# Mirrored spectral weights by a gather from GpSimd in place of a mirrored copy in DRAM, in a two-layer spectral and FFN kernel

## The chip, the cores and the metric

The kernel runs on one core of one Trainium2 chip. The metric is device time in microseconds, the median of several runs. A profiled execution is one further run; its span is the time between the first and the last recorded event on the core.

## The reference

The input x has 2048 rows (positions) of 448 features in bf16. Two kinds of layer alternate, A, B, A, B, each with a residual:

```
x = x + A(layernorm(x));  x = x + B(layernorm(x))      # twice, same weights
A(x):  X = rfft2(x);  X = X * (w_r + 1j*w_i);  return irfft2(X)      # w: [2048, 225]
B(x):  h = relu(x @ w1 + b1)**2;  return h @ w2 + b2                 # 448 -> 1792 -> 448
```

The rfft runs over the features (225 frequencies, number 0 is not needed here because the layernorm takes out the mean), the full FFT over the 2048 positions. The weights of A are indexed by position frequency k (2048 rows) and feature frequency l.

## The kernel before, in words

**Stages of A.** The 2048-point transform is split as 32 x 64. Stage A (`first_A`, `second_A`) multiplies 16 tiles of 128 positions by a small matrix `FA` that also carries the layernorm's 1/std, and gives the components of 32 residues in `XA`. Because the input is real, residue k1 and residue 32-k1 are conjugates, so that the stages after it work on 16 pairs p: residues p and 32-p, and for p=0 the residues 0 and 16. The groups of pairs (`GROUPS`, one or two pairs each) go through four steps:

- `stage_TD`: the transform over the features, by `TD_sb` in the first layer and, on half the length, by `TQ_sb` in the second; every product needs all 16 tiles in `XA`. The result is copied from PSUM into `U`.
- `stage_B`: the 64-point transform with twiddle factors, by the table `G_sb`; copied into `EF`, as residue p and residue 32-p side by side.
- `stage_W`: the complex multiplication by the weights, on VectorE: two products (`tmp` <- `EF` times `Wa`, and times `Wb`), then a sum and a difference into `Z`.
- `stage_Bi`: the inverse 64-point transform by the table `H_sb`, copied into `VT`.

`stage_TI` and `stage_AI` go back over the features and the residues and add the residual, `ln_B` computes the second layernorm, a DMA transpose gives `yT`, and `h_rows` and `o_tile` are the FFN. Then the second layer follows.

**The weights.** `Wa` holds real over imaginary parts on the two halves of the partitions, `Wb` the other way round. Partition q holds rows 32q+k of w. For the residue 32-p, row 32-p is needed and q runs backwards. So the kernel before first writes a mirrored copy of half the weights to DRAM, `Wrev` (16 x 64 rows of 224), with two DMAs on SP, and `load_W` then reads rows p from w and rows 32-p from `Wrev`, in rows of 224 bf16, 448 bytes. It does that in three `RANGES` of p, with G and H cut in the same way, all from SP's queue. The weights lie in buffers that are otherwise `x_sb` and `xin` (`Wa` of first and second layer) and `yT` (`Wb`), so that they are loaded anew for the second layer, in between the transposes of the FFN.

**The order of the work.** The author's `_Sched` records every operation with its reads and writes, gives each engine a list order from assumed costs, priorities (`PR`) and choices of engine (`EN`: a letter per step, `a` ScalarE, `d` VectorE, `p` GpSimd, other letters a choice), and puts in semaphore waits. The engines then follow their lists strictly. DMAs on SP made before `sch.chain = None` keep the order in which they are written. `warm_fn` puts products of ones where PE would stand.

**Lines of the profile.** L577 is every matrix product, L617, L618 are copies on ScalarE and on VectorE or GpSimd, L635 is every VectorE operation on two tensors (the weights' products among them), L572 every plain DMA, L567 the transposes, L1104 the products of ones. `DIRECT` names pairs that skip the sum and difference in `stage_W` and use twice as many products in `stage_Bi` in their place: 14 and 15 in the second layer. In the profile `xr` appears as `VT`, `U`, `EF`, `Z` and the FFN's hidden rows as `arena`, `Wb` as `yT`, the first `Wa` as `x_sb`, the second as `xin`.

Of the kernel before, what the change touches and what calls it, by code (L numbers as in the profile page):

```python
# [10 lines left out]
P = 128  # L11
S = 2048
D = 448
# [10 lines left out]
DIRECT = ((), (14, 15))  # L24
GROUPS = ((1,), (0,), (2, 3), (4, 5), (6, 7), (8, 9), (10, 11), (12, 13), (14, 15))
RANGES = ((0, 4), (4, 10), (10, 16))
# [10 lines left out]
def make_constants():  # L37

    comp = np.zeros((32, 32))
    hi = np.arange(32)
    comp[0] = 1.0
    comp[1] = np.cos(np.pi * hi)
    for p in range(1, 16):
        comp[2 * p] = np.cos(2 * np.pi * p * hi / 32)
        comp[2 * p + 1] = -np.sin(2 * np.pi * p * hi / 32)
    FA = np.zeros((32, 4, 32, 4))
    for j in range(4):
        FA[:, j, :, j] = comp.T  # L50
    FA = FA.reshape(P, P)
    FI = FA.T.copy()

    dd = np.arange(HD)[:, None]
    l = np.arange(1, 225)[None, :]
    th = 2 * np.pi * l * (dd - 223.5) / D  # L60
    TD = np.zeros((2, 2, P, LW))
    for g, M in enumerate((np.cos(th), -np.sin(th))):
        TD[g, 0] = M[:P]
        TD[g, 1, 32:] = M[P:]
    TD = TD.transpose(2, 0, 1, 3)


    th = 2 * np.pi * np.arange(1, 225)[None, :] * (np.arange(QD)[:, None] - 223.5) / D
    TQ = np.zeros((QD, 2, 2, QD))
    for g, M in enumerate((np.cos(th), -np.sin(th))):  # L70
        TQ[:, g, 0] = M[:, 1 - g::2]
        TQ[:, g, 1] = M[:, g::2]


    m = np.arange(64)
    lo = (m % 4) * 16 + m // 4
    k2 = np.arange(64)
    G = np.zeros((P, NP, 2, 192))
    H = np.zeros((P, NP, 2, 256))
    for p in range(NP):  # L80
        for q in range(2):
            k = (p if p or not q else 16) + 32 * k2
            th = 2 * np.pi * lo[:, None] * k[None, :] / float(S)
            c, n = np.cos(th), np.sin(th)
            if p:
                C, Dm = np.concatenate([c, n]), np.concatenate([-n, c])
            else:
                z = np.zeros_like(c)
                C, Dm = (np.concatenate([a, z] if q == 0 else [z, a]) for a in (c, -n))
            G[:, p, q] = np.concatenate([-Dm, C, Dm] if p == 0 or q == 0 else [Dm, C, -Dm], 1)  # L90
            K, N = c.T, n.T
            if p:
                b = np.concatenate([-N, K, N, -K], 1)
                H[:, p, q] = np.concatenate([b, -b if q == 0 else b])
            else:
                for g, b in enumerate((np.concatenate([K, N], 1), np.concatenate([-N, K], 1))):
                    H[:, p, g, q * P:(q + 1) * P] = np.concatenate([b, -b if g == 0 else b])


    l0 = np.arange(1, 225)[:, None]  # L100
    cl = np.where(l0 == 224, 1.0, 2.0) / (S * D)
    th = 2 * np.pi * l0 * (np.arange(HD)[None, :] - 223.5) / D
    TI = np.zeros((QD, 2, 2, HD))
    for g, M in enumerate((cl * np.cos(th), cl * np.sin(th))):
        for r in range(2):
            TI[:, r, g] = M[r::2]

    return dict(FA=np.concatenate([FA, -FA], 1), FI=np.concatenate([FI, -FI], 1), TD=TD, G=G, H=H, TI=TI, TQ=TQ,
                J=np.eye(P)[::-1])
# [82 lines left out]
def _pages(ap):  # L192
# [12 lines left out]
    p0 = ap.offset // row if row else 0  # L205
    halves = range(p0 // 64, (p0 + pat[0][1] - 1) // 64 + 1)
    return [(name, int(i), h) for i in pg for h in halves]


class _Sched:  # L210

    ENGINES = ("pe", "act", "dve", "pool", "sp")
    NDSEM = {"sp": 20, "pool": 16, "act": 8, "pe": 0, "dve": 0}
    DMA_RATE = 400.0
    SWITCH = 95.0
    STICK = 3000.0

    def __init__(self):
        self.ops = {e: [] for e in self.ENGINES}
        self.units = []
        self.last_write = {}
        self.reads_since = {}
        self.bias = 0.0
        self.look = dict.fromkeys(self.ENGINES, 0.0)
        self.chain = None
        self.warm_fn = None
# [5 lines left out]
    def add(self, eng, fn, reads=(), writes=(), is_dma=False, cost=100.0, lat=130.0, unit=None):  # L235
# [22 lines left out]
        if unit is not None:  # L258
            u = unit
        elif tile is not None and tile.unit is not None:  # L260
            u = tile.unit
        else:
            u = _Unit(eng, tile)
            u.bias = self.bias
            u.seq = len(self.units)
            if is_dma and eng == "sp" and self.chain is not None:
                u.after, self.chain = self.chain or None, u
            self.units.append(u)
            if tile is not None:
                tile.unit = u  # L270
# [30 lines left out]
    def schedule(self):  # L301
# [32 lines left out]
        cand = {e: [] for e in self.ENGINES}  # L334
        bank_free = [0.0] * NB
        bank_user = [None] * NB
        dma_free = 2300.0

        ready = {}
        best = {}  # L340
# [154 lines left out]
def bass_interleave_layers__spectral_gfnet__dense_activation_squared_relu__prompt_kernel(nc, A_x, A_w_r, A_w_i, B_x, B_w1, B_b1, B_w2, B_b2, out):  # L495
# [6 lines left out]
    with ExitStack() as es:  # L502
# [179 lines left out]
        def load_W(W, f, p0, p1):  # L682

            for i in range(2):
                rows, w = slice(64 * (i ^ f), 64 * (i ^ f) + 64), w_dram[i]
                dma("sp", W[rows, p0:p1, 0, :], w[:, p0:p1, 1:225])
                if p0 == 0:
                    dma("sp", W[rows, 0:1, 1, :], w[:, 16:17, 1:225])
# [494 lines left out]
```

## Time and profile before

| | us |
|---|---|
| median of 9 runs | 278.81 |
| lowest and highest | 277.25, 280.34 |
| profiled execution | 278.24 |
| span of its profile | 276.4 |
| busy PE | 259.1 (94%) |
| busy PE, loading weights | 168.7 (61%) |
| busy DVE (VectorE) | 206.8 (75%) |
| busy ACT (ScalarE) | 176.9 (64%) |
| busy POOL (GpSimd) | 9.6 (3%) |

PE is TensorE. Matmuls overlap, so a busy PE isn't PE at its best rate. HBM was read for 18.02 MB and written for 2.75 MB. In the profile `[5.03 <-DMA X]` after an instruction is the time for which its engine stood idle before it and what ended that time; a line of waits gives who waited, for whom, the sum, the number of times and the longest. A chain of waits follows the work that ended last back to what released it.

### The profile page before, as it was taken

The numbers are of one execution on the slowest core, as the hardware profiler recorded it, in microseconds if no ns is written. First come the engines' busy times: TensorE is split into PE (matmuls) and PEld (weight loads), VectorE is DVE, ScalarE is ACT, GpSimd is POOL, SyncE is SP. The second block draws the span as 40 slices with busy tenths as digits, with TensorE's granted clock in tenths as the row PEclk, the third lists the DMA queues.
The fourth block names the chain that finished last, engine by engine and source line by source line (L and its number), as shares of the span: only waits on it lengthen the run. The fifth ranks groups of instructions, "written<-read, shape, count | busy, mean of one in ns | idle before, by whom it ended". The sixth has DMA issues, their size and how long they took to land.

```text
span 276.4 us, 6385 instructions
## 1 busy us (share of the span) xinstructions
PE 259.1 (94%) x2385; PEld 168.7 (61%) x2385; DVE 206.8 (75%) x686; ACT 176.9 (64%) x366; POOL 9.6 (3%) x23
## 2 busy tenths in 40 slices
PE   7699669999998999999999999899999999999995
PEld 2479647879654444554458799769754554554454
DVE  3876467599999999898689698599999865212542
ACT  5797826899747976324815789899856795001820
POOL 2740000000000000000000000000000000000000
PEclk9799968999999999999999999999999999999999
DMA  7969999902233424202230400002332600111001
GB/s 236 311 143 264 279 219 314 318 4 47 62 54 69 82 38 105 55 0 63 52 88 6 96 2 4 0 4 40 21 75 62 142 2 8 42 50 36 0 23 46
DMA packets 42969, 23.92 MB, mean 87 GB/s; under 512 B 35164, under 2 KB 41660, under 8 KB 42940
## 3 DMA queue, kind: packets, MB, share of 16 engines
q1 hardware_dynamic: 41996, 22.77, 34.1%
q10 hardware_dynamic: 944, 0.75, 0.8%
q8 instruction: 19, 0.31, 0.5%
q14 instruction: 10, 0.08, 0.1%
HBM read 18.02 MB, written 2.75 MB: 75 GB/s over the span
## 4 chain that ended last, share of the span: by engine, by line
PE 66%; SPq 13%; DVE 7%; ACT 7%; DMA 3%; issue 2%; DVEq 0%; ACTq 0%
PE ps L577 66%; SPq L572 13%; ACT VT L617 3%; DMA yT<-Wrev 2%; ACT tmp L617 2%; ACT arena L617 2%; DVE tmp L635 1%; DMA yT<-xin 1%; DVE x_sb L912 1%; DVE x_sb L910 1%; ACT yT L617 1%; DVE arena L635 1%; DVE xin L644 1%; DVE XA L618 0%; DVE st L928 0%
## 5 line engine op out<-in xcount | busy, mean ns | idle before, releaser
L600 ACT ACTIVATE arena<-ps,b1T 128x512 bf16<-128x512 f32 (+1 forms) x140 | 73.7, 615 | 30.8 <-PE ps L577 30.6
L577 PE MATMUL ps<-yT,W_sb 64*128 64x512 bf16 (+1 forms) x980 | 86.1, 333 | 1.2 <-DMA yT<-xin 0.9
L577 PE MATMUL ps<-W_sb,arena 128*128 128x448 bf16 (+1 forms) x476 | 87.1, 341 | 0.0
L577 PEld LDWEIGHTS ps<-yT,W_sb 64*128 64x128 bf16 x980 | 49.8, 94 | 37.2 <-issue 1.8
L577 PEld LDWEIGHTS ps<-W_sb,arena 128*128 128x128 bf16 x476 | 46.0, 98 | 37.2 <-DVE arena L635 0.8
L635 DVE TENSOR_TENSOR arena<-arena 128x512 bf16<-128x512 bf16 (+1 forms) x140 | 47.9, 367 | 15.4 <-ACT arena L600 15.1
L1009 DVE TENSOR_TENSOR x_sb<-ps,arena 128x448 bf16<-128x448 f32 (+1 forms) x34 | 20.2, 595 | 23.7 <-PE ps L577 23.4
L617 ACT ACTIVATE arena<-ps 128x896 bf16<-128x896 f32 (+1 forms) x32 | 25.9, 865 | 11.2 <-PE ps L577 11.2
L600 ACT ACTIVATE mv<-mv,epst 128x2 f32<-128x2 f32 (+1 forms) x42 | 12.1, 298 | 21.0 <-DVE mv L737 19.3
L577 PE MATMUL ps<-arena,G_sb 128*128 128x224 bf16 x128 | 16.7, 285 | 5.0 <-DMA G_sb<-c_G 5.0
L716 ACT ACTIVATE VT<-x_sb 128x448 bf16<-128x448 bf16 x24 | 13.7, 570 | 11.1 <-DVE x_sb L912 11.1
L577 PE MATMUL ps<-H_sb,arena 128*128 128x128 bf16 x272 | 17.9, 224 | 0.7 <-DVE arena L635 0.6
L577 PEld LDWEIGHTS ps<-H_sb,arena 128*128 128x128 bf16 x272 | 16.7, 101 | 1.6 <-DVE arena L635 1.5
L577 PEld LDWEIGHTS ps<-arena,G_sb 128*128 128x128 bf16 x128 | 13.2, 108 | 6.3 <-DMA G_sb<-c_G 5.3
L617 ACT ACTIVATE VT<-ps 128x512 bf16<-128x512 f32 x29 | 15.4, 644 | 1.9 <-PE ps L577 1.8
L635 DVE TENSOR_TENSOR arena<-tmp 128x896 bf16<-128x896 bf16 (+1 forms) x30 | 16.2, 587 | 0.1
L617 ACT ACTIVATE XA<-ps 128x512 bf16<-128x512 f32 x25 | 13.9, 598 | 3.5 <-PE ps L577 3.5
L617 ACT ACTIVATE tmp<-ps 128x896 bf16<-128x896 f32 (+1 forms) x18 | 14.3, 850 | 2.2 <-PE ps L577 2.2
L1104 PE MATMUL ps<-ones 128*128 128x512 bf16 x40 | 12.3, 436 | 2.0 <-POOL ones L648 1.9
L635 DVE TENSOR_TENSOR tmp<-arena,yT 128x896 bf16<-128x896 bf16 (+1 forms) x15 | 8.7, 588 | 6.2 <-DMA yT<-Wrev 6.2
L644 DVE TENSOR_SCALAR xin<-x_sb,mv,rstd 128x512 bf16<-128x512 bf16 x32 | 11.6, 405 | 0.0
L577 PE MATMUL ps<-Fs,xin 128*128 128x256 bf16 x32 | 9.0, 303 | 2.5 <-POOL Fs L629 2.2
(74 smaller groups left out, 262.9 us busy)
## 6 DMA issues: line engine op xcount, KB each, us to landing
W_sb<-in_B_w_dram SPq DMA_DIRECT2D x2, 896.0 KB, 10.1
out_dram<-x_sb SPq DMA_DIRECT2D x15, 112.0 KB, 1.7
W_sb<-in_B_w_dram SPq DMA_DIRECT2D x1, 1568.0 KB, 14.2
H_sb<-c_H SPq DMA_DIRECT2D x2, 768.0 KB, 7.7
yT<-Wrev SPq DMA_DIRECT2D x8, 168.0 KB, 5.2
G_sb<-c_G SPq DMA_DIRECT2D x2, 576.0 KB, 8.3
xin<-in_A_x_dram SPq DMA_DIRECT2D x2, 448.0 KB, 5.7
x_sb<-Wrev SPq DMA_DIRECT2D x4, 168.0 KB, 8.9
```

Of the source, the lines that this page charges most:

```text
L572: return e.dma_start(o, i)
L577: op = sch.add("pe", lambda e: e.matmul(_res(o), lhsT, rhs, start=start, stop=stop, skip_group_check=skip), [lhsT, rhs], [o], cost=max(_fr ...
L600: sch.add("act", lambda e: e.activation(o, _res(i), func, **kw), rd, [o], cost=c)
L617: op = sch.add("act", lambda e: e.activation(o, _res(i), ACT.Copy) if h[0].eng == "act" else e.tensor_copy(o, _res(i)), [i], [o], cost=c[" ...
L635: sch.add(eng, lambda e: e.tensor_tensor(o, _res(a), b, op), [a, b], [o], cost=_free(o) / rate + 69.0)
L644: sch.add(eng, lambda e: e.tensor_scalar(o, i, s1, s2, op0=op0, **kw), rd, [o], cost=_free(o) / 3.84 + 50.0 + (10.0, 80.0, 140.0)[len(rd) ...
L716: sch.add("act", lambda e: e.activation(o, x, ACT.Square, accum_out=sd[:, t, 1:2]), [x], [o, sd[:, t, 1:2]], cost=560.0)
L910: sch.add("dve", lambda e, xx=xx, xi=xi, r=r: e.tensor_tensor(xx, _res(r), xi, ALU.add), [r, xi], [xx], cost=536.0)
L912: small(lambda e, xx=xx, xi=xi, r=r, i=i: e.scalar_tensor_tensor(out=xx, in0=_res(r), scalar=1.0, in1=xi, op0=ALU.mult, op1=ALU.add, accum ...
L1009: sch.add("dve", lambda e: e.tensor_tensor(o, _res(i), xb[:, t, d0:d1], ALU.add), [i, xb[:, t, d0:d1]], [o], cost=(d1 - d0) / 0.96 + 69.0)
L1104: return lambda e: e.matmul(ps[:, b, :], ones[:], ones[:, None, :].to_broadcast([P, 4, P]), start=True, stop=True)
```

## The change

- `Wrev` and its two DMAs go. `load_W` now copies whole runs of consecutive rows, `WC` = 225 elements each, into one row of 33 slots per partition, and gets the mirrored rows by `gather`: an indirect DMA from GpSimd, each of 64 partitions by 8 rows of w (1800 elements), whose row numbers come from the constant list `back` (63 down to 0, times 4, plus 3 or 2). Eight gathers load the first layer's weights, eight the second's.
- Since runs of w aren't turned about in p, the mirrored residues of a group stand in reverse: `stage_B` writes them so, `stage_W` reads the weights with a hand-built access pattern and turns them back in the sum and difference. Rows start at p x 225 + 1, so every other one starts at an odd element.
- G has one table per p, shared by both residues (192 columns, not 2 x 192), H 384 columns (not 512). `DIRECT` is gone. p=0 goes last, there are two `RANGES`.
- In the second layer `stage_TD` writes adjacent PSUM columns, and the copy to `U` interleaves them (before: a step of 2 in PSUM).
- FA comes first on ACT's DMA queue, J and b1 come after the first range. `A2`'s scratch moves from `xin` to `VT`. All of `PR` and `EN` and some assumed costs are new, so that each engine's order is new too. On GpSimd the first eight gathers now stand between the reversed copies of tiles 10 and 11 and of tiles 6 and 7.

```diff
-DIRECT = ((), (14, 15))
-GROUPS = ((1,), (0,), (2, 3), (4, 5), (6, 7), (8, 9), (10, 11), (12, 13), (14, 15))
-RANGES = ((0, 4), (4, 10), (10, 16))
+GROUPS = ((1,), (2, 3), (4, 5), (6, 7), (8, 9), (10, 11), (12, 13), (14, 15), (0,))
+RANGES = ((1, 6), (6, 16))
+WC = 225
+HQ = 384
...
+    dc["back"] = nc.inline_tensor((4 * (63 - m) + np.array([[3, 2]])).astype(np.uint32), name="c_back").ap()
...
-        G_sb = sb("G_sb", [P, NP, 2, 192])
-        H_sb = sb("H_sb", [P, NP, 2, 256])
+        G_sb = sb("G_sb", [P, NP + 1, 192])
+        H_sb = sb("H_sb", [P, 15 * HQ + 4 * P])
...
+        def gather(o, i, h):
+            idx = bass.IndirectOffsetOnAxis(back[:, h:h + 1], 0)
+            sch.add("pool", lambda e: e.indirect_dma_start(o, None, i, idx), [back[:, h:h + 1]], [o], is_dma=True, cost=1000.0,
+                    lat=2.0 * 64 * 8 * WC / sch.DMA_RATE)
...
-        Wrev = [nc.dram_tensor(f"Wrev{i}", (16, 64, LW), BF16, kind="Internal").ap() for i in range(2)]
-        for i in range(2):
-            dma("sp", Wrev[i], (A_w_r, A_w_i)[i].rearrange("(q k) l -> k q l", k=32)[16:32, ::-1, 1:225], writes=[f"Wrev{i}"])
...
+            a, b = (0, p1) if p0 == 1 else (p0, 17)
             for i in range(2):
-                rows, w = slice(64 * (i ^ f), 64 * (i ^ f) + 64), w_dram[i]
-                dma("sp", W[rows, p0:p1, 0, :], w[:, p0:p1, 1:225])
-                if p0 == 0:
-                    dma("sp", W[rows, 0:1, 1, :], w[:, 16:17, 1:225])
+                dma("sp", W[64 * (i ^ f):64 * (i ^ f) + 64, a * WC:b * WC], w_dram[i][:, a * WC:b * WC])
+            h = 0 if p0 == 1 else 1
             for i in range(2):
-                rows = slice(64 * (i ^ f), 64 * (i ^ f) + 64)
-                r, p = Wrev[i].rearrange("k r l -> r k l"), max(p0, 1)
-                dma("sp", W[rows, p:p1, 1, :], r[:, 16 - p:16 - p1:-1, :], reads=[f"Wrev{i}"])
+                j = 64 * (1 - (i ^ f))
+                gather(W[j:j + 64, WC * (25 - 8 * h) + 1:WC * (33 - 8 * h) + 1], w_rows[i], h)
...
-                            l0 = g * LW + ((1 - g) if k == 0 else g)
-                            o, x, w = slice(l0, l0 + LW - 1, 2), x[0:QD], TQ_sb[:, g, k, :]
+                            l0 = 256 * g + QD * ((1 - g) if k == 0 else g)
+                            o, x, w = slice(l0, l0 + QD), x[0:QD], TQ_sb[:, g, k, :]
...
-                tt(T[:, f], X, W[:, p:p + n], ALU.mult)
+                a = W[:, p * WC + 1:p * WC + 1 + LW]
+                a = bass.AP(tensor=a.tensor, offset=a.offset, ap=[list(a.ap)[0], [WC, n], [WC * (34 - 2 * p - n) + 1 if p else WC * 16, 2],
+                                                                  [1, LW]])
+                tt(z.rearrange("p q (f s) l -> p f q s l", f=2)[:, f] if p == 0 else T[:, f], X, a, ALU.mult)
...
-            tt(z[:, 0:2], T[:, :, :, 0], T[:, :, :, 1], ALU.add)
-            tt(z[:, 2:4], T[:, :, :, 0], T[:, :, :, 1], ALU.subtract)
+            for i, op in enumerate((ALU.add, ALU.subtract)):
+                tt(z[:, 2 * i:2 * i + 2], T[:, :, :, 0], T[:, :, ::-1, 1], op)
...
-                        w = xin[:, t, 0:D].rearrange("p (g d) -> p g d", g=2)
+                        w = VT[:].rearrange("p a b t c j -> p (a b t c j)")[:, 512 * t:512 * t + D].rearrange("p (g d) -> p g d", g=2)
```

## The prediction, made before the changed kernel ran

> **What bounds the kernel now.** I read the 40 slices first, for a resource that is full while PE is not:
>
> ```profile
> PE   7699669999998999999999999899999999999995
> ...
> DMA  7969999902233424202230400002332600111001
> GB/s 236 311 143 264 279 219 314 318 4 47 62 54 69 82 38 105 55 0 63 52 88 6 96 2 4 0 4 40 21 75 62 142 2 8 42 50 36 0 23 46
> DMA packets 42969, 23.92 MB, mean 87 GB/s; under 512 B 35164, under 2 KB 41660, under 8 KB 42940
> ```
>
> A slice is 6.9 us. For the first eight, up to 55 us, the transfers are full and PE has its only deep hole (a 6); after that PE is at 9 and DMA idles. 35164 of 42969 packets are under 512 bytes: the rows of weights are 448. Next the waits from 20 to 60 us, for who stands in the hole:
>
> ```profile
> DVE tmp L635 <- DMA yT<-Wrev: 6.2, 2, 3.5
> PEld ps L577 <- DMA G_sb<-c_G: 5.3, 1, 5.3
> PE ps L577 <- DMA G_sb<-c_G: 5.0, 1, 5.0
> ```
>
> Then PE's timeline, first stage and (from 154.19) second stage, for what the hole costs:
>
> ```profile
> 29.77 2.46 PE L577 MATMUL ps<-TD_sb,XA 128*128 128x224 bf16 x24
> 37.27 4.66 PE L577 MATMUL ps<-arena,G_sb 128*128 128x224 bf16 x24 [5.03 <-DMA G_sb<-c_G]
> 41.72 3.59 PE L577 MATMUL ps<-H_sb,arena 128*128 128x128 bf16 x48
> ...
> 51.75 1.69 PE L577 MATMUL ps<-TI_sb,VT 112*128 112x224 bf16 x16 [0.46 <-ACT VT L617]
> ...
> 154.19 2.46 PE L577 MATMUL ps<-TQ_sb,XA 112*128 112x112 bf16 x24 [0.33 <-DVE XA L618]
> ...
> 176.84 1.32 PE L577 MATMUL ps<-TI_sb,VT 112*128 112x224 bf16 x16 [0.45 <-ACT VT L617]
> ...
> 180.00 0.95 PE L577 MATMUL ps<-TI_sb,VT 112*128 112x112 bf16 x16
> 180.89 0.93 PE L577 MATMUL ps<-tmp,FI_sb 128*128 128x448 bf16 x4
> ```
>
> After the 5.03 us wait the 24 G products start 190 ns apart; undisturbed ones start 97 ns apart. The windows say why: the granted clock is 0.58 and 0.50 of full in 36 to 42 us. So a starved PE pays twice. The first spectral stage, from its first TD product (21.21 us) to the first TI (51.75), takes 30.5 us; the second, whose weights are already on the chip, 154.19 to 176.84, **22.65 us**. The difference, 7.9 us, is the transfers' price.
>
> What bounds the second stage? Its two windows, with busy us of PE, PEld, DVE, ACT, POOL, then clock, DMA share and GB/s:
>
> ```profile
> 154.20:165.00 10.80, 10.80 (x125) 10.80 (x126) 8.87 (x18) 8.53 (x12) 0.00 (x0) 1.00 0.07 16
> 165.00:176.80 11.80, 10.76 (x153) 9.54 (x150) 9.43 (x17) 11.47 (x20) 0.00 (x0) 1.00 0.01 2
> ```
>
> PE first, then ACT (11.47 of 11.80): near balance, so one engine relieved gains little, and in stage one ACT is what is late next once the transfers are gone.
>
> **What the Trainium skill says.** "DMA: Bandwidth & Descriptors", Specifications: line rate needs transfers of at least 512 B. The trace agrees: 193 to 272 GB/s at a DMA share of 1.0 in 33 to 42 us, where 448-byte rows move, against 386, 380 and 341 in 45 to 54 us with long rows. The same page, same table: a DMA from GpSimd has its first byte after about 1 us, one from SP about 0.6; and, Anatomy of one DMA, about 2.0 us fixed for the whole transfer. No run here has a DMA from GpSimd. "GPSIMD Engine Reference", 2.1: the first call of a freshly loaded routine may cost about 6 us, and (section 8) GpSimd shares SBUF interfaces with VectorE; the trace shows neither. "Vector Engine (DVE) Microarchitecture Reference", 5.1: 4-byte alignment makes no difference to the double-rate mode of two-source operations; the trace has no such odd start, so it can't confirm it.
>
> **The change, part by part.**
>
> *Transfers.* Gone: 0.9 MB written to Wrev at the start and as much reading of input; about 0.73 MB of G and 0.49 MB of H. Up to the second range of weights it leaves 1.9 MB (x, FA), 0.23 (TD), 0.84 (G), 0.49 (first H), 1.96 direct weights, 1.84 gathered: 7.3 MB, in runs of 2700 to 4950 bytes (weights) or longer than 512. At 320 GB/s, under the 341 to 386 of the long rows, from 2.3 us: all landed at 25 us, the rest of H (1.1 MB) at 29, the FFN weights (another 3.9 MB) at 41. Needed: first weights about 3 us after TD begins, the second range about 8 us after, the FFN at about 52. So each has 5 us or more; at 200 GB/s they would be late by about 8. On SP 49 issues ahead of the FFN become 26, at some 0.6 us each; the 1.98 and 3.12 us issues behind Wrev have no cause left. I take the DMA wait and the cold clock out of the stage altogether.
>
> *Stage one without it.* Template 22.65 us. Of it, DIRECT's 16 extra H products (55 ns each, 0.9 us PE) are absent, its two saved DVE operations (0.53 each) are present: they nearly cancel. p=0 goes last and leaves 8 H products at the tail, not 16. I take **22.2 us**, bounds 21 to 24.
>
> *The eight first gathers, on POOL's queue.* This is the price. The order of instructions shows POOL doing five small pieces, then eight gathers, then the reversed copy for tiles 6 and 7. Behind that copy wait PE's tiles 6 and 7, queued ahead of tiles 12 to 15; every TD product needs all sixteen. Before, POOL's copy of tiles 8 to 11 began at 7.47 us, on x landing. After it come a scaling and a second copy (0.53, 0.47, 0.53 us): gathers from 9.0. The price of one: no less than SP's shortest issue, 0.43 us; at most the 2.0 us of a whole transfer, if POOL were held for it, beside the 6 us of a first call. I take 1.1, just over the page's 1 us. So 9.0 + 8 x 1.1 = 17.8; copy 0.55, 18.35; six tiles of five products at 111 ns, 3.3, 21.65; evacuation and first TD, 0.9 us as before (20.33 to 21.21): **TD at 22.6**. It was 21.21: 1.4 us lost. DVE gives a floor: 13 statistics at 0.56 us, nine scalings at 0.25, two XA evacuations and small operations are some 15 us from 4.1, with 1.5 of waits 20.6. FA now issued first hides nothing of that: it removes PE's wait for the first Fs (2.2 us), which isn't last.
>
> First TI: 22.6 + 22.2 = 44.8, against 51.75: **-6.95 us**.
>
> *Second stage.* TQ now writes adjacent PSUM words: 64 products at 94 ns (24 in the 2.26 us up to the next piece, 156.45) become like the TI products of the same size with adjacent output, 16 in 180.00 to 180.89, 56 ns: -2.4 us of PE; H -0.9. PE is then no longer first. DVE gains 1.1. ACT and DVE then hold 20.0 + 19.4 = 39.4 us, 19.7 each, with about 1.5 us of lead and tail 21.2. U's evacuation now writes every second element: I take no charge, since XA's, in runs of four, take 0.51 us for 512 elements against 0.47 for 448 dense; at worst double, 9 x 0.81 us over two engines, +3.6. I take **-1.1 us**, bounds -2 to +3.6.
>
> *Weights at odd starts.* 14 products of 896 elements per stage. At double rate nothing; [...]+0.46 each, 6.5 us of DVE per stage. I take nothing, by the page.
>
> *FFN and second loads.* 28 SP issues become 8, and 8 gathers go to idle POOL. SP's transposes of tiles 8 to 15 now stand behind the yT weight loads, which wait for PE's h of chunk 1. Between chunk 1 and chunk 2 PE has 84 products at 190 ns, 16 us; the four issues (2.5), two transposes (2.5 each: five took 12.72 from 79.14) and a landing (3.2) need 10.7: hidden by 5 us, and without that cover it would show in full. The first gathers wait for the row list `back`, issued fourth on SP and due well before 9 us. PE's FFN work is the same: 0, give or take 1. A2's scratch moved to VT and the x weights earlier: they weren't waited for, 0.
>
> **Sum** -6.95 - 1.1 = -8.05 us. The profiled execution, span 276.4, took 278.24; the median of nine is 278.81, 0.57 higher. On the median: 278.81 - 8.05 = **270.8**. Half a per cent, 1.4 us, is about what can be told from no change.
>
> **The rivals.**
> - *Gathers dearer, at 1.5 us (chance 0.18).* TD at 9.0 + 12 + 0.55 + 3.3 + 0.9, plus 1.7 for a partly cold clock: 27.5; first TI 49.7: -2.1 - 1.1, **275.6**. For it: the price is unseen and DVE is busy on a shared SBUF interface. Against: POOL otherwise is idle.
> - *Gathers become the bound (0.09).* [...]the six tiles run at half clock, 6.6 us. Break-even is TD at 30.65: (30.65 - 9.0 - 0.55 - 6.6 - 0.9)/8 = 1.7 us each. At 2.3: TD 35.5, TI 57.7, +5.9 - 1.1: **283.6**, slower.
> - *Odd starts halve DVE (0.05).* DVE 19.4 + 6.5 = 25.9, stage about 28: TI 50.6 (-1.15), second +5.3: **283**.
> - *Transfers still last (0.08).* At 200 GB/s the stage loses about 5 of its 8 us again: **275.8**. Against: the long-row windows.
> - *The forecast (0.60),* own range 265.5 to 273.5: floor TD 20.6, stage 21.5, second -2.
>
> **Numbers.** The rivals at 275.6 and 275.8 spill a little into no change. Of their 0.26, 0.21 is faster by over 0.5% and 0.05 is not: faster 0.60 + 0.21 = 0.81, same 0.05, slower 0.09 + 0.05 = 0.14. The range leaves out the slower cases and a little at each end: 265.5 to 277.0.
>
> **What would show it.** POOL: about 1.1 us between gathers, the copy of tiles 6 and 7 near 18. PE: TD near 22.6, no wait on G, clock 1.00 from 25 to 45, TI near 45, TQ under 75 ns. DVE products at 0.62 us. DMA full until 41, not 55. It is wrong if that copy comes after 25, if DVE waits for a gather, or if tmp products take over 0.7 us.

## The result, and the profile after

The changed kernel takes **281.61 us** (median of 10 runs, 280.72 to 282.21) where the kernel before takes 278.92 beside it (31 runs): a ratio of **1.0091, 95% interval 1.0066 to 1.0117**. It is 0.9% slower; 270.8 was forecast, with a range of 265.5 to 277.0. The profiled execution took 281.88 us, span 280.1.

The five places that the prediction used divide the spans:

| stretch | before | after | forecast | change |
|---|---|---|---|---|
| start to first TD | 21.21 | 33.76 | 22.6 | +12.55 |
| first TD to first TI (first stage) | 30.54 | 22.29 | 22.2 | -8.25 |
| first TI to TQ (FFN and what follows it) | 102.44 | 101.63 | no change | -0.81 |
| TQ to TI (second stage) | 22.65 | 22.83 | 21.55 | +0.18 |
| the rest | 99.56 | 99.59 | no change | +0.03 |

So the transfers did what was forecast, and more than all of it was lost again ahead of the first TD. The slices of the page, 7.0 us each:

```profile
PE   7494999999999999999999898999999999999996
...
PEclk9686899999999999999999999999999999999999
DMA  7999993000562357020200000002026500101011
GB/s 225 276 273 256 249 374 115 2 0 4 108 146 52 95 102 178 5 66 4 67 0 2 0 2 4 0 2 41 2 47 137 110 0 2 49 33 35 0 35 49
DMA packets 25450, 22.05 MB, mean 79 GB/s; under 512 B 16364, under 2 KB 22988, under 8 KB 25292
```

DMA is full until about 42 us, where it was 55, with 25450 packets for 42969. But PE's hole, 6s in slices 5 and 6 before, has moved ahead of TD: there are now 4s in slices 2 and 4 (7 to 14 and 21 to 28 us). PE's own line shows it, and what it costs (start, length, then in brackets how long PE stood and for whom):

```profile
20.26 0.27 PE L589 MATMUL ps<-Fs,m 128*128 128x256 bf16 x1
20.37 0.38 PE L1111 MATMUL ps<-ones 128*128 128x512 bf16 x1
24.55 0.37 PE L589 MATMUL ps<-Fs,xin 128*128 128x256 bf16 x1 [3.80 <-ACT XA L629]
...
33.76 2.08 PE L589 MATMUL ps<-TD_sb,XA 128*128 128x224 bf16 x20 [0.18 <-issue]
...
56.05 1.73 PE L589 MATMUL ps<-TI_sb,VT 112*128 112x224 bf16 x24 [0.26 <-ACT VT L629]
...
157.68 1.34 PE L589 MATMUL ps<-TQ_sb,XA 112*128 112x112 bf16 x24 [0.35 <-ACT XA L629]
...
180.51 1.73 PE L589 MATMUL ps<-TI_sb,VT 112*128 112x224 bf16 x24 [0.26 <-ACT VT L629]
```

No G product waits any more. But PE stands 3.8 us for ScalarE's evacuation (the copy of its results from PSUM), and the tiles after 24.55 run at half clock, products 213 ns apart and not 109: in 24 to 30 us the granted clock is 0.50. The line gives the stretch, its length, the busy us of PE, PEld, DVE, ACT and POOL, then clock, DMA share and GB/s:

```profile
24.00:30.00 6.00, 5.45 (x26) 3.94 (x27) 1.02 (x4) 3.86 (x8) 0.00 (x0) 0.50 1.03 260
```

Then POOL's line:

```profile
10.60 0.56 POOL L630 COPY VT<-xin 128x448 bf16<-128x448 bf16 x1 [2.49 <-DMA xin<-in_A_x_dram]
...
12.28 1.08 POOL L585 DMA_INDIRECT x_raw<-in_A_w_r_dram,back  x1 [0.17 <-issue]
13.67 0.91 POOL L585 DMA_INDIRECT x_raw<-in_A_w_i_dram,back  x1 [0.30 <-issue]
...
20.95 0.90 POOL L585 DMA_INDIRECT yT<-in_A_w_i_dram,back  x1 [0.30 <-issue]
21.85 0.57 POOL L630 COPY VT<-xin 128x448 bf16<-128x448 bf16 x1
```

A gather follows the other after 1.2 us, priced at 1.1. They start at 12.3 and not 9.0, since x (tiles 8 to 11) lands at 10.5 and not 7.5: ahead of them stand the copies of tiles 10 and 11, from 10.60, and of tiles 8 and 9, from 11.55. And the line for whom PE stood, ScalarE:

```profile
19.06 0.50 ACT L640 ACTIVATE Fs<-FA_sb,rstd 128x256 bf16<-128x256 bf16 x1
23.80 1.09 ACT L629 ACTIVATE XA<-ps 128x512 bf16<-128x512 f32 x2 [4.24 <-remote]
```

This is the odd one. ScalarE's copy needs products that PE began at 19.28 to 20.26. It starts at 23.80, and the trace names nobody for the wait ("remote"). In the raw records of the trace, PE's increments for these products are written between 23.65 and 23.95, in one burst. The products ended from 19.55 to 20.53, so each increment is 3.4 to 4.1 us late. So three theories of the 12.5 us, with the cold clock as a consequence of any:

- **Late x.** SP no longer stands behind Wrev; TD, G and the weights follow x at once and share the 16 DMA engines with it. Worth about 3 us (10.5 against 7.5).
- **POOL's queue.** The copy of tiles 6 and 7 stands behind eight gathers (the prediction's own price).
- **Late signals.** While POOL makes gathers, the semaphore increments of the other engines arrive late.

### The profile page after: what moved, and what is told of

It reads as the page before. It is cut to its first block, busy times and chain, and to the rows that moved or that the text cites. A ratio compares the mean times of both kernels' runs of the same rounds, so it can differ in the third digit from the quotient of the medians.

```text
span 280.1 us, 6369 instructions
## 1 busy us (share of the span) xinstructions
PE 262.8 (94%) x2390; PEld 165.2 (59%) x2390; DVE 211.4 (75%) x696; ACT 178.3 (64%) x369; POOL 19.2 (7%) x28
## 2 busy tenths in 40 slices
DMA packets 25450, 22.05 MB, mean 79 GB/s; under 512 B 16364, under 2 KB 22988, under 8 KB 25292
## 4 chain that ended last, share of the span: by engine, by line
PE 81%; ACT 7%; DVE 4%; DMA 3%; another core or an unknown queue 2%; issue 1%; POOL 0%; ACTq 0%; DVEq 0%
PE ps L589 79%; ACT arena L629 3%; DMA xin<-in_A_x_dram 3%; PE ps L1111 2%; ACT XA L629 1%; ACT tmp L629 1%; DVE arena L647 1%; DVE tmp L647 1%; ACT VT L629 1%; ACT Fs L640 0%; DVE x_raw L922 0%; DVE tmp L630 0%; DVE st L940 0%; ACT mv L612 0%
## 5 line engine op out<-in xcount | busy, mean ns | idle before, releaser
L1021 DVE TENSOR_TENSOR x_raw<-ps,arena 128x448 bf16<-128x448 f32 (+1 forms) x34 | 20.0, 594 | 22.5 <-PE ps L589 22.5
L629 ACT ACTIVATE arena<-ps 128x896 bf16<-128x896 f32 (+1 forms) x33 | 27.8, 965 | 2.5 <-PE ps L589 2.5
L612 ACT ACTIVATE mv<-mv,epst 128x2 f32<-128x2 f32 (+1 forms) x42 | 12.3, 303 | 24.2 <-DVE mv L745 20.0
L1111 PE MATMUL ps<-ones 128*128 128x512 bf16 x61 | 20.1, 460 | 1.9 <-POOL ones L660 1.9
L629 ACT ACTIVATE VT<-ps 128x512 bf16<-128x512 f32 x29 | 17.2, 712 | 2.4 <-PE ps L589 2.4
L724 ACT ACTIVATE VT<-x_raw 128x448 bf16<-128x448 bf16 x24 | 14.1, 597 | 4.4 <-DVE x_raw L924 4.4
L589 PEld LDWEIGHTS ps<-H_sb,arena 128*128 128x128 bf16 x256 | 15.0, 98 | 3.2 <-DVE arena L647 2.8
L647 DVE TENSOR_TENSOR tmp<-VT 128x224 bf16<-128x224 bf16 (+1 forms) x56 | 16.4, 316 | 0.0
L589 PE MATMUL ps<-arena,G_sb 128*128 128x224 bf16 x128 | 14.3, 259 | 0.6 <-ACT arena L629 0.5
L629 ACT ACTIVATE tmp<-ps 128x896 bf16<-128x896 f32 (+1 forms) x15 | 12.3, 871 | 2.7 <-PE ps L589 2.7
L744 DVE BATCH_NORM_STATS2 st<-xin 128x6 f32<-128x448 bf16 x13 | 7.6, 612 | 6.4 <-DMA xin<-in_A_x_dram 6.4
```

Of the source, the lines that this page charges most:

```text
L589: op = sch.add("pe", lambda e: e.matmul(_res(o), lhsT, rhs, start=start, stop=stop, skip_group_check=skip), [lhsT, rhs], [o], cost=max(_fr ...
L612: sch.add("act", lambda e: e.activation(o, _res(i), func, **kw), rd, [o], cost=c)
L629: op = sch.add("act", lambda e: e.activation(o, _res(i), ACT.Copy) if h[0].eng == "act" else e.tensor_copy(o, _res(i)), [i], [o], cost=c[" ...
L647: sch.add(eng, lambda e: e.tensor_tensor(o, _res(a), b, op), [a, b], [o], cost=_free(o) / rate + 69.0)
L724: sch.add("act", lambda e: e.activation(o, x, ACT.Square, accum_out=sd[:, t, 1:2]), [x], [o, sd[:, t, 1:2]], cost=560.0)
L744: small(lambda e, si=si, xi=xi: e.bn_stats(si, xi), [xi], [si], _free(xi) / 0.96 + 69.0)
```

## The experiments

All are edits of the changed kernel, made in the finished lists of the engines where possible, so that nothing else is reordered. They are shown shortened, with comments where code is left out. In each the first stage takes 22.3 us and the second 22.8 unless another number is given; so the first TD tells nearly all. They ran on four chips, here called 4, 10, 13 and 14; which one the changed kernel itself ran on is not on record. "Held" in the table means that the weights wait until x has landed.

| run | median us | ratio to before (95%) | first TD |
|---|---|---|---|
| changed kernel | 281.61 | 1.0091 (1.0066 to 1.0117) | 33.76 |
| copy ahead of gathers | 282.14 | 1.0108 (1.0059 to 1.0156) | 33.63 |
| SP's plain DMAs | 276.68 | 0.9899 (0.9851 to 0.9947) | 29.00 |
| weights held for x | 281.28 | 1.0077 (1.0046 to 1.0108) | 33.65 |
| plain DMAs, held | 280.50 | 1.0060 (1.0037 to 1.0083) | 31.86 |
| plain DMAs, held, b1 early | 274.63 | 0.9845 (0.9795 to 0.9894) | 26.34 |
| small dummy gathers | 284.15, one run | - | 34.71 |
| full dummy gathers | 281.84, one run | - | 32.96 |
| gathers at the start | 277.17 | 0.9948 (0.9917 to 0.9978) | 28.91 |

### Is it POOL's queue?

```diff
         sch.schedule()
+        pq = sch.ops["pool"]
+        last = [op for op in pq if not op.is_dma][-1]      # reversed copy of tiles 6 and 7
+        pq.remove(last)
+        pq.insert([op.is_dma for op in pq].index(True), last)
```

> The changed kernel with one edit: on GpSimd the reversed copy of tiles 6 and 7 stands ahead of the eight gathers, not behind them. Three theories for the 12.5 us that the stretch before the first TD lost (21.21 to 33.76). Queue: TensorE waited for that copy at 21.85; then with the copy near 12.5 the XA evacuations flow, only the 3 us of the late x are left, TD comes near 24 to 26 and the time is 272 to 275. Signals: while GpSimd makes its gathers, the other engines' semaphore updates arrive late (TensorE's of 19.3 to 20.3 were seen at 23.65); then TensorE still stands until the gathers end, TD stays at 30 or later and the time at 279 to 282. Late x alone (tiles 8 to 11 landed at 10.54, not 7.5): no change from 281.6.

282.14 us, TD at 33.63. The copy is done at 13.3, nine us earlier, and PE and ScalarE stand as before, even longer:

```profile
25.53 0.37 PE L589 MATMUL ps<-Fs,xin 128*128 128x256 bf16 x1 [5.09 <-ACT XA L629]
```

The queue theory falls. PE's list in the changed kernel agrees: ten tiles (50 products) follow the stand, tiles 2, 3, 8 and 9 first and then 6 and 7, so that PE stood four tiles ahead of the copy's readers. The next kernel has no gathers in the first layer:

```diff
         # for each of the first eight gathers, behind its range's direct weights
+        sch.ops["pool"].remove(op)
+        op.eng, op.fn = "sp", lambda e: e.dma_start(o, rows)    # 64 runs of 3600 bytes, plain
+        sq.insert(sq.index(anchor) + 1, op)
```

> The changed kernel, the first layer's eight gathers taken off GpSimd: SP fetches the same number of bytes by eight plain DMAs, each behind the direct weights of its range. It leaves out the mirroring in the first layer: these rows come in ascending, not descending order of q. Queue and signals both: TensorE no longer stands near 20.7 to 24.6, no cold clock, only the 3 us of the late x are left: TD near 24 to 25, time 271 to 274. If it ends at 272 while the copy put ahead of the gathers ends near 281, the gathers themselves hold the others up; if both end alike, it was only the queue. Late x alone: 281.

276.68 us, TD at 29.00: 4.8 us earlier, with the same bytes and the same copy for tiles 6 and 7. PE's stand of 3.8 us is gone. But not the 24 to 25 that I expected; PE waits for something else, which no theory had named:

```profile
20.18 0.18 PE L593 MATMUL ps<-J_sb,arena 14*128 14x14 bf16 x1 [1.53 <-DMA arena<-in_B_b_dram]
```

That is b1's little product. It stands among the tiles in PE's list, and b1 is now loaded behind the first weights.

### Late x, and late b1

```diff
+        sq[5].deps.extend(sq[0:3] + aq[1:3])      # first G (and all SP work behind it) waits for x
```

> The changed kernel, with SP's DMA of the first part of G and all weights behind it held until all of x has landed; the gathers stay as they are. Late x: with the 16 DMA engines to itself x lands by 7 to 8 us as before the change, GpSimd's copy of tiles 8 and 9 starts near 7.7, not 10.6, gathers start near 9.2 and all that follows comes 3 us earlier: TD near 30.5, time 278 to 279. If x's landing isn't what starts the gathers, or what is lost comes from the gathers alone, no change from 281.6. If the held weights then come late, up to 285.

281.28, TD 33.65. x landed at 9.5, gathers began at 11.2, a microsecond earlier, and nothing came of it: the b1 product now ran at 20.64, since b1 was held too. With plain DMAs in place of the gathers:

> Both edits: eight plain DMAs of SP for the gathers (rows of the first layer unmirrored, which is left out), and SP's DMAs of G and weights held until x has landed. If late x and the gathers' place together are the whole loss of 12.5 us, TD comes back to 21 to 22.5 and the time to 269 to 271, which is what the blind sum gave. If the second stage's missing gain or something else in the stretch counts too, it stays above 272.

280.50, a miss, worse than without the hold: 4.45 us of wait for b1 and half clock behind it. So b1 was moved:

```diff
+        for op in (j_op, b1_op): sq.remove(op)
+        sq[3:3] = [j_op, b1_op]                   # right behind x; TD held with the rest
```

> The kernel with SP's plain DMAs for the first layer's gathers (rows unmirrored, mirroring of the first layer left out) and with the weights held until x has landed, with one more edit: J and b1 are loaded directly behind x, ahead of TD, and TD is held too. Before it TensorE stood 4.5 us for b1 in the middle of the tiles (at 21.55), then ran at half clock until 25.2. Theory that b1, moved behind the weights by the change, is a third part of the loss: first TD at 26 to 26.5, not 31.86, time near 275. Theory that the late x, b1 and the gathers are all of it: TD at 21.5 to 23, time 270 to 272. If b1's wait only hides another (scalings, statistics): TD over 30, time over 279.

274.63 us, TD at 26.34: the first theory to the digit. x in time and b1 in time are together worth 2.7 us against the kernel with plain DMAs (29.00), b1 alone 5.5 where the hold had made it last. This is 1.5% faster than the kernel before; but its first layer's rows are not mirrored.

```profile
17.13 0.18 PE L593 MATMUL ps<-J_sb,arena 14*128 14x14 bf16 x1
...
26.34 2.08 PE L593 MATMUL ps<-TD_sb,XA 128*128 128x224 bf16 x20 [0.18 <-issue]
```

### Do gathers delay signals that have nothing to do with them?

To the kernel with plain DMAs (TD 29.00), eight gathers are added into a scratch tile that no one reads, behind all of POOL's copies:

```diff
+            d = _Op("pool", lambda e: e.indirect_dma_start(scr_part, None, table, rows), True, 0.0, 0.0)
+            sch.ops["pool"].insert(pos + n, d)    # 64 rows of 32 bytes, or of 3600
```

> The kernel with SP's plain DMAs for the first layer's gathers (rows unmirrored), and added to it eight gathers from GpSimd into a scratch tile that nobody reads, 64 rows of only 32 bytes each, at the place on GpSimd's queue where the copy put ahead had them. If the making of descriptors on GpSimd is what holds the other engines' signals up, first TD comes near 33 and not at 29.0, time near 281. If it is the gathers' bytes, or waiting for their data, TD stays at 29 and the time near 277.

> As the one with small dummy gathers, but with 64 rows of 3600 bytes each, the size of the real ones; nobody waits for them. If gathers hold signals up, whoever needs them, TD near 33, time near 281 or over it, since 1.84 MB more are moved. If only a wait for their data or their place on GpSimd's queue cost the time, TD at 29 to 30, time 277 to 278.

With 32 bytes a row TD comes at **34.71**, with 3600 at **32.96** (its first stage takes 23.1 us), against 29.00 without. 16 KB in all cost 5.7 us, 1.8 MB 4.0: it isn't the bytes. Each is one run, on chip 10, where the kernel without dummies ran on chip 4. Which of the two costs more they can't tell, since TD differs by as much between profiles of one and the same order (32.67 to 34.32 with the changed kernel's list). POOL is as long busy for a small gather as for a full one (0.90 us in both); its line in the kernel with small dummies:

```profile
14.77 0.91 POOL L1135 DMA_INDIRECT scr<-in_A_w_i_dram,back  x1 [0.30 <-issue]
...
22.02 0.90 POOL L1135 DMA_INDIRECT scr<-in_A_w_i_dram,back  x1 [0.30 <-issue]
```

And PE's line in the same kernel, where it stands for others though none of them waits for a dummy:

```profile
23.34 0.28 PE L595 MATMUL ps<-Fs,xin 128*128 128x256 bf16 x1 [2.25 <-DVE Fs L647]
26.00 0.37 PE L595 MATMUL ps<-Fs,xin 128*128 128x256 bf16 x1 [1.44 <-DVE b1T L657]
```

The raw records say the same. From 8 to 24 us, increments that the engines' instructions carry / increments that the trace has a record for:

```
                       PE          ACT         DVE
before               108 / 108    29 / 29     46 / 46
changed kernel        31 / 21     18 / 8      44 / 15
plain DMAs            42 / 42     22 / 22     46 / 46
small dummies         30 / 15     16 / 5      35 / 17
```

Where POOL makes gathers, a third to two thirds of the records come after the window or not at all; without them each is there. That signals are late, and not only their records, rests on the times: ScalarE and PE stand as long as the records are late, and the medians move with TD (276.68 against 281.61). Two rivals remain to be named. GpSimd could slow the other engines' own work over a shared interface, as the prediction feared; but VectorE's statistics take 0.61 us both in the changed kernel and with plain DMAs. And the recording itself could have a part in it; span and clock are on record for every run, so no run here shows what happens with no recording at all.

### Does it always happen?

A kernel made for the second stage (below) has the gathers in the same place, and showed the opposite: it took 275.85, its TD came at 28.22, ScalarE's copy at 20.84, right behind the products, and no record was missing (49/49, 24/24, 47/47), though POOL made its gathers from 12.99 to 22.60:

```profile
21.63 0.97 POOL L585 DMA_INDIRECT yT<-in_A_w_i_dram,back  x1 [0.31 <-issue]
22.61 0.60 POOL L630 COPY VT<-xin 128x448 bf16<-128x448 bf16 x1
```

ScalarE in the same kernel:

```profile
20.84 1.14 ACT L629 ACTIVATE XA<-ps 128x512 bf16<-128x512 f32 x2 [0.46 <-PE ps L589]
```

So on that chip the gathers show no cost: TD at 28.22 is no later than the 29.00 without them, and the copy behind the gathers, at 22.61, held nobody. Its lists up to the first TI are the changed kernel's. It had run on a third chip, 14. So both were run on one chip, a fourth, 13, with one edit for both (plain DMAs for the FFN's transposes, which leaves the FFN's input untransposed):

```diff
-                fn = lambda e: e.dma_start_transpose(o, i)
+                fn = lambda e: e.dma_start(o, i.rearrange("p (m c) -> p m c", c=P))
```

> The changed kernel with plain DMAs of the same tiles in place of the FFN's DMA transposes (it leaves out the transposition of the FFN's input, after the first stage); all that comes before the first TI is as in the changed kernel. If the gathers hold up signals on every chip: first TD near 33.8, TensorE standing after 20.3, time near 281.6 if the FFN takes as long. If it is the chip that makes the difference, and this chip is like the third one: TD near 28.2, time near 276; then the next kernel too shows TD near 28.

> The same with the shortened sum and difference of pairs 14 and 15 in the second layer (their result left out for the most part, the FFN's input not transposed). If the chip makes the difference, its first TD is within 1 us of the kernel beside it, and its time is below it by what the two operations are worth, 0 to 1.2 us; if the program does, TD is near 28.2 here and near 33.8 in the kernel beside it.

281.77 and 281.69 (ratios 1.0082 and 1.0079), TD at 34.32 and 34.06: the one that had taken 275.85 is as slow as the other. **It is not the program.** Nor is it that one execution: the three kernels through DRAM below ran on chip 14 too, with gathers in the FFN, and in all four profiles from it PE's records from 100 to 135 us are complete, while in each of the 15 profiles with such gathers from elsewhere 17 to 25 of some 279 are missing. So three chips (4, 10 and 13) hold signals up and one did not. What differs between them was not found.

### Gathers in another place

```diff
+        sq.remove(back_op); sq.insert(0, back_op)  # row list first on SP
+        sq[4:4] = [j_op, b1_op]                    # right behind x; TD and the rest held for x
+        pq[2:2] = gathers                          # ahead of all copies of GpSimd
```

> The changed kernel (FFN's input not transposed, plain DMAs in place of the transposes, as in the kernel that took 281.77 with first TD at 34.32) with another place for the gathers: the row list is SP's first DMA, and GpSimd makes the eight gathers from about 2.9 us on, ahead of all its copies; J and b1 stand right behind x, TD and the weights are held until x has landed. If it is signals held up while the tiles are worked on that cost, the gathers are over at 12.5, when x has just landed, nothing stands at 20 to 24, and TD comes at 25 to 27, time 273 to 275. If the gathers' bytes make x late instead (1.84 MB, 6 us at 300 GB/s): x at 13 to 15, TD 28 to 30, time 276 to 278. If GpSimd's own copies and scalings, now at 13 to 16, hold the tiles: TD over 30.

277.17 us, ratio **0.9948 (0.9917 to 0.9978)**, on a chip that holds signals up. The gathers run from 2.95 to 12.44 and again hold records up (of VectorE's 23 increments from 6 to 11 us, 8 are recorded there), but now in a stretch in which the engines would be waiting for x:

```profile
2.95 1.04 POOL L585 DMA_INDIRECT x_raw<-in_A_w_r_dram,back  x1 [1.13 <-DMA back<-c_back]
...
11.54 0.90 POOL L585 DMA_INDIRECT yT<-in_A_w_i_dram,back  x1 [0.30 <-issue]
```

PE's first tile in it:

```profile
13.70 0.37 PE L589 MATMUL ps<-Fs,xin 128*128 128x256 bf16 x1 [6.97 <-POOL Fs L641]
```

TD comes at 28.91, 3.8 and 5.0 us earlier than in two kernels with the gathers in the old place on the same chip (32.67 and 33.89, both from the section on the second stage), 5.4 earlier than on another (34.32). Not all of it need be the place: with plain DMAs, x and b1 in time alone were worth 2.7. TD is not at 25 to 27, as PE's first tile waits for GpSimd's scaling, itself behind the gathers, until 13.7. It is the best kernel found that gathers every row: the changed kernel with three list edits, and faster than both. It has the FFN's transposes as plain DMAs too, which leaves the FFN's input untransposed; in time that edit is worth nothing that can be measured (1.0082 with it, 1.0091 without).

The same without fillers: five of the products of ones ahead of TD are dropped, and the 13 in the second stage.

```diff
+        pe[a:b] = [op for op in pe[a:b] if op.unit is not None]   # from the second stage's first TQ product to its first TI
+        for op in nine[4:]: pe.remove(op)                         # the run of products of ones ahead of TD
```

> Both edits (gathers at the start; no products of ones in the second stage), and five of the nine products of ones behind the third tile dropped. As the first of these three, less what the fillers are worth: 0 to 1 us in the second stage, 0 to 1.8 us ahead of TD: 271 to 275 if the place of the gathers was the cause. If the fillers are needed for the clock, it is slower than the first.

276.73, TD 28.94, the same within the intervals: these fillers, ahead of TD, were not what was late.

### Through DRAM again, in long runs

A mirrored copy like the one before the change, but with whole runs to read:

```diff
+        e.dma_start(Wrev[n], w_rows[n].rearrange("(q a) x -> a q x", a=4)[2:4, ::-1, :])   # [2, 64, 1800]
```

> A kernel that computes all of it, with no gather in the first layer: SP writes the mirrored rows of w to DRAM as before the change, but in runs of 8 rows (3600 bytes, not 448), and loads them by plain DMAs where the gathers were; J and b1 are loaded directly behind x; the row list behind b2. 1.84 MB more are moved. Theory that gathers, late x and late b1 are the loss: no gather, b1 in time, x late (10.5 or a little over, since the mirrored copy runs beside it): TD at 27 to 28, first stage 22.3, time 275 to 277. If the copy through DRAM makes the weights late as before the change, the stage takes 25 to 30 us and the time is over 279.

Then the copy held for x (as in the diff of the held weights), and that without five products of ones ahead of TD too:

> The one with long mirrored rows through DRAM, and the mirrored copy (with TD and all weights behind it) held until x has landed. If it is late x that is left: x lands near 9.4, TD at 26.3 as with plain DMAs, b1 early and the hold, time 274 to 275.5. If the hold makes the weights late: stage over 23 us, time over 277.

> The held one with long mirrored rows, and five of the nine products of ones behind the third tile dropped. They ran at half clock from 11.5 to 15.3 in the kernel with b1 early, while the scalings for the next tile were done at 13.4. If the fillers are what is late there, the fourth tile starts at 13.4 to 13.6 and TD comes 1 to 1.8 us earlier, time 272.5 to 274. If the tiles wait for scalings and statistics further on, TD stays at 26 and the time does not change.

291.19, 293.47 and 294.37 us (ratios 1.042, 1.048, 1.053): misses, all three. The first stage takes 36 us. From 14 to 28 us DMA moves 88 GB/s at a share of 0.27:

```profile
14.00:28.00 14.00, 11.86 (x84) 7.87 (x82) 7.39 (x31) 8.40 (x19) 0.00 (x0) 0.94 0.27 88
```

The Trainium skill, "DMA: Bandwidth & Descriptors", section "Why a DMA increments its semaphore by 16 and not by 1" (its paragraph on how many engines), offers a reason: the outermost step that is larger than 1 sets how many DMA engines take part, and mine has 2. The share of 0.27 agrees. The remedy is k outermost (16), in rows of 450 bytes:

> No gather in the first layer: as the kernel with mirrored rows through DRAM, but the mirrored copy is made in rows of 450 bytes with k outermost (16 of them) as before the change, and only read as whole runs of 3600 bytes; J and b1 right behind x; the FFN's input not transposed, as in the two beside it. If the copy in long runs lost because its two outermost steps put it on few of the 16 DMA engines (their share was 0.3 from 14 to 28 us): TD at 24 to 26.5, first stage 22.3 to 24, time 273 to 277. If the way through DRAM itself makes the weights late: TD over 26.5 or a stage over 25 us, time over 279.

279.74 (ratio 1.0010, 0.9983 to 1.0038): TD at 26.03 as hoped, but a first stage of 27.74; SP issues no load of a mirrored row before 17.44, when the copy has landed (with long runs, 27.88). The DMA share while the copy runs is over 1 now:

```profile
12.00:18.00 6.00, 5.84 (x26) 2.66 (x25) 4.73 (x28) 4.30 (x13) 0.00 (x0) 0.76 1.12 186
```

So with 16 outermost steps 8.2 of the 13.7 us that the stage had lost came back, though the copy's runs are shorter, and the way through DRAM keeps 5.5.

### The second stage

The forecast had -1.1 us; it got 0.2 longer. One part undone:

```diff
-                            l0 = 256 * g + QD * ((1 - g) if k == 0 else g)
-                            o, x, w = slice(l0, l0 + QD), x[0:QD], TQ_sb[:, g, k, :]
+                            l0 = g * LW + ((1 - g) if k == 0 else g)
+                            o, x, w = slice(l0, l0 + LW - 1, 2), x[0:QD], TQ_sb[:, g, k, :]
...
-            if first:
                 evac(U[:, p:p + n, :], q[lambda b: ps[:, b:b + n, 0:2 * LW]], "TDe")
-            # else: the copy that interleaves
```

> The changed kernel with one part undone: in the second layer the TQ products write in steps of 2 in PSUM as before, and the copy to U is dense. Theory that ScalarE and VectorE bound the second stage: TensorE's TQ products take 94 ns again (+2.9 us busy), which replaces products of ones, and ScalarE's copies to U take 0.92 us, not 1.16 to 1.34 (-2.0 us in all): the stage gets 0.5 to 1.5 us shorter, 280.2 to 281.1. Theory of the prediction, that the adjacent writes gained and something else took it back: the stage gets 1 to 2.4 us longer, 282.6 to 284. No difference if the two cancel: 281.6.

283.10 (ratio 1.0144), the stage **24.04** us and not 22.83. So the adjacent writes did gain, 1.2 us net, and my theory that they gain nothing is wrong. Net, because the interleaving copy costs: ScalarE's copies of 896 elements to U take 1.16 to 1.34 us, dense ones 0.92. It is no clock: that is 1.00 throughout in both. Then VectorE's share, the two operations that DIRECT had saved:

```diff
-                tt(z[:, 2 * i:2 * i + 2], T[:, :, :, 0], T[:, :, ::-1, 1], op)
+                # second layer, p == 14: the same on 2 of 224 frequencies
+                sch.add("dve", lambda e, a=args, op=op: e.tensor_tensor(*[v[..., 0:2] for v in a], op), ...)
```

> The changed kernel; in the second layer the sum and the difference of pairs 14 and 15 are taken over 2 of 224 frequencies only, so that the result for these pairs is left out for the most part. It takes back the two operations that the loss of DIRECT gave VectorE (0.62 us each). If VectorE's own list bounds the second stage (it can hand nothing of its products to ScalarE), the stage from TQ to TI takes 21.6 to 21.9, not 22.8. If ScalarE or the tail of p=0 bounds it, it stays at 22.5 to 22.9.

The stage takes 22.66 (again 22.67 in the run on chip 13): VectorE is busy 0.8 us less (the two operations still take 0.16 us each and not 0.62), which is worth 0.15. VectorE alone doesn't bound it. And TensorE's fillers, the changed kernel without the 13 products of ones of this stage:

> The changed kernel (FFN's input not transposed) without the 13 products of ones in the second layer's stage, 2.8 us of TensorE's time at 216 ns. If TensorE bounds that stage with its fillers, they stand where a real product could run, and the stage is 1 to 2 us shorter (21 to 21.8, not 22.8), time 280 to 280.8. If the products wait for ScalarE's and VectorE's copies anyway, the stage stays within 0.3 us of 22.8 and the time at 281.7. If the clock falls without them, it gets longer.

281.86, the stage 24.04, longer, but with the clock at 0.90 from 170 to 176 us and 0.82 from 176 to 182:

```profile
170.00:176.00 6.00, 3.75 (x50) 3.41 (x49) 5.77 (x11) 4.70 (x10) 0.00 (x0) 0.90 0.02 4
176.00:182.00 6.00, 5.31 (x72) 5.14 (x70) 3.49 (x7) 3.63 (x7) 0.00 (x0) 0.82 0.00 0
```

It isn't the work: in the kernel with gathers at the start and the same 13 left out, the clock stayed at 1.00 and the stage took 22.79, what it takes with them (22.81). So the fillers cost nothing; whether they hold the clock, two profiles that differ can't say. What took the other 1.4 us (1.2 gained, 0.2 lost) was not shown. The engine that no run relieved by itself is ScalarE. The changed kernel's two windows show it nearly full in the first (10.43 of 10.80 us), and VectorE in the second (11.34 of 12.00):

```profile
157.70:168.50 10.80, 10.23 (x138) 9.20 (x139) 9.10 (x17) 10.43 (x14) 0.00 (x0) 1.00 0.01 2
168.50:180.50 12.00, 10.92 (x133) 8.14 (x131) 11.34 (x22) 10.20 (x17) 0.00 (x0) 1.00 0.01 2
```

ScalarE and VectorE together hold 20.63 + 20.45 = 41.1 us, where the forecast had 39.4. That they are the bound is likely, not shown; p=0 as last group is untried.

## Why the prediction was wrong, point by point

- **First TD at 22.6: wrong, and nearly the whole error.** 33.76 was measured, +11.2 us. The step that failed is the path: "behind that copy wait PE's tiles 6 and 7". PE never waited for that copy. It stood four tiles earlier for ScalarE, whose signals from PE came 3.4 to 4.1 us late while gathers were made; the sum put at nothing what gathers do to engines that don't wait for them. That costs 4.8 us (33.76 to 29.00; 5.7 and 4.0 with dummies), on three chips of four, and nothing by the place in the queue. Two more terms failed. "Gathers from 9.0": x landed 3 us late, and b1, which the change moves behind the first weights, was in no term at all; in time, both are worth 2.7 us (29.00 to 26.34). "Six tiles of five products at 111 ns": ten tiles were left behind the stand, the first 27 products 213 ns apart. Some 3.7 us (26.34 against 22.6) are not taken apart; x still lands 1.9 us later in that kernel than in the one before.
- **1.1 us a gather: right** (1.2 apart), by luck in part: it was taken from a latency to the first byte, and SP's shortest issue takes 0.33 us, not 0.43. The rival "gathers become the bound" had the sign, at 2.3 us each, and a TD of 35.5; its mechanism, a gather too dear on POOL, is not what happened.
- **First stage 22.2: right** (22.29, from 30.54). No wait for G or for a gather; DMA full until 42, forecast 41.
- **FA first "hides nothing": right**, and beside the point: what matters in that queue is that x now has company.
- **Second stage -1.1: wrong by 1.3**, a size. TQ fell to 49 ns a product, under the 75 given; "I take no charge" for the copy to U was a mis-sized term (+0.24 to +0.42 us on each), and so was "DVE gains 1.1" (it gained 2.15, 18.30 to 20.45). The even split of work over ScalarE and VectorE would give 0.4 us for the 0.8 taken off VectorE; 0.15 was measured.
- **Odd starts free: right.** The products take 0.62 us, before and after. The page that I drew on, "Vector Engine (DVE) Microarchitecture Reference", 5.1, holds here.
- **FFN no change: right within its 1 us** (-0.8), though two of its readings were off: a transpose issue takes 1.2 to 2.0 us, since the 12.72 us for five hold waits as well. The gathers there cost nothing measurable: the stretch takes 101.37 on the chip without late signals, 101.36 on another.

The sum: +11.16 (TD) + 0.09 (first stage) - 0.81 (FFN) + 1.28 (second) + 0.03 = 11.75, which is what lies between -8.05 and the +3.7 of the spans.

## What to carry to other kernels

Work that goes to an idle engine's queue can still cost the busy ones: add it as a dummy that nobody waits for, and see whether the rest slows, before blaming the queue. When a change removes what held a DMA queue back, price what now starts earlier beside the first loads, and every small load that slips behind big ones. And a stand that the trace can put to nobody is worth a second chip.

## What the runs showed of the hardware that was not expected

- While GpSimd makes indirect DMAs (0.90 us each, 1.2 apart, 64 rows, the same for rows of 32 and 3600 bytes), semaphore increments of PE, ACT and DVE come late or have no record, PE's up to 4.1 us late, on three of four chips. How is open; that the bytes don't matter is shown by two single runs (16 KB and 1.8 MB).
- In the FFN, where DMA is nearly idle, such gathers cost no time, though records are missing there too on the same chips (257 of 278 of PE's from 100 to 135 us).
- While a DRAM-to-DRAM copy with 2 outermost steps ran, DMA moved 88 GB/s at a share of 0.27; with 16 steps the share was 1.12.
- Behind PE's stand of 3.8 us the clock was 0.50 from 24 to 30 us.
